# First pair's preparation reordered over queues and engines, second pair's casts placed two steps later

## The chip, the cores and the metric

The kernel runs on one core of one Trainium2 chip. A core has the engines TensorE (PE in the profile, with its weight loads PEld), VectorE (DVE), ScalarE (ACT), GpSimd (POOL) and SyncE (SP), each with its own queue of instructions in program order, and 16 DMA engines that carry out the transfers that SP, ACT and POOL issue. The metric is the device time of one execution in microseconds (us), lower is better.

## The reference

Three parts run one after the other. First an attention over B = 2 batches, H = 8 heads, S = 768 positions and D = 64 columns a head, in which a query sees only the keys of its own hash bucket (six sign bits of a projection):

```python
q_bits = (einsum('bhsd,dk->bhsk', q, proj) > 0)      # k_bits likewise
mask = q_bucket[:, :, :, None] == k_bucket[:, :, None, :]
scores = where(mask, (q @ k^T) / sqrt(D), -1e9)
attn = softmax(scores)                               # rows of 768
out = attn @ v                                       # then laid out as 1536 tokens x 512
```

Then a dense MLP, x = silu(x @ w_in) @ w_out (512 to 2048 to 512), and then a choice of one of eight experts for the tokens with x @ w_skip > 0, whose result is added to x. The change touches only the attention, and of it only the start.

## The kernel before, in words

The heads are handled in pairs: pair i has two heads, hd 0 and hd 1, and there are 8 pairs. Each pair's queries are cut in two halves of 384; a half of a pair is a unit (`units`, L367), and a unit has three blocks of 128 queries (qt) for each of the two heads. One block of one head is a step; there are 96 steps, 12 to a pair. Step 0 to 2 are hd 0 of the first unit and steps 3 to 5 its hd 1; from step 6 on heads alternate, so step 12 is hd 0 and step 13 hd 1 of pair 1 (L369, L370).

float32 products are made from float32r parts. Per pair there are four operand tiles (`prep_alloc`, L291), each with a plane for each head. With r the 64 partitions that belong to the head and o the other 64 (`own`, L296): K1 holds K's high part in r ("kh", a cast) and its low part in o ("kl"); Q1 holds Q's high part in r ("qa") and a copy of it in o ("qb"); Q2 holds Q's low part ("ql") and 24 rows of bucket marks; K2 holds a copy of K's high part ("k2") and rows of marks. `prep_op` (L303) makes each of these for one pair and head on the engine that it is given; for pairs other than the first, "k2" and "qb" are transfers that SP issues from one part of SBUF to another. `prep_proj` (L332) projects raw K and Q with four matmul groups and turns the signs into marks (tile mb, on DVE), and `prep_rows` (L343) copies the marks with SP's transfers into Q2 and K2: four for the first pair, six for the others. "scale" (L307) scales the next pair's raw K on ACT.

A step s runs: `em_S`, two matmuls over Q1 and K1 (all 128 partitions) and two over Q2 and K2 (88), into a PSUM tile of which there are two; `em_soft`, the maximum (mx, L395) and a bias (bs, L397) on DVE and the exp on ACT (L399); two steps later `em_T`, six transposes of the exp's result (L411), copied out by ACT (L414, first half) and DVE (L416, second half); and in odd steps from the middle of the next unit on `em_PV` (L425). `em_r` (L432) takes a unit's sums, transposes them, writes them out (r_d, L439) and reads them back broadcast (rb, L442, two transfers), all issued by SP.

The order of the work is written out by hand in the loop at L523. In a step it emits em_S of s, the first half of em_T of s - 2, the operations of `PRE` due in this step (the next pair's "kh" and "qa" on ACT), em_PV, em_soft, the second half of em_T, em_r, and then the operations of `POST` due (the next pair's "k2" and "qb" by SP, "kl" and "ql" on POOL), prep_rows, and raw and v loads. The index m of a step in its pair decides what is due; for the first pair (i == 0) PRE and POST have lists of their own. em_r of unit 0 falls on step 9, prep_rows of pair 1 on step 8 and its prep_proj on step 5. A queue keeps program order, and SP waits in it for the data of each transfer.

Ahead of the loop (L472 to L514) stand the constants' load (ct, by ACT), the raw loads of pair 0 head by head (k, q, k, q by SP), 29 matmuls on zeros (`em_busy`), the projection of hd 0 alone (pd, L491), the operands of hd 0 and most of hd 1, then the loads and rows.

Of the kernel before, what the change touches and what calls it, by code (L numbers as in the profile page):

```python
# [25 lines left out]
def kernel(  # L26
# [237 lines left out]
    def attention(hook):  # L264
# [11 lines left out]
        def prep_load(i):  # L276

            b, p = divmod(i, NP)
            raws[i] = [topp.tile([P, S], F32, name="raw", tag=tag, bufs=2) for tag in "kq"]
            for hd in range(2) if i == 0 else (None,):  # L280
                for t, src in zip(raws[i], (kT, qT)):
                    if hd is None:
                        nc.sync.dma_start(t, src[b, 2 * p:2 * p + 2].rearrange("h d s -> (h d) s"))
                    else:
                        nc.sync.dma_start(t[own(hd)], src[b, 2 * p + hd])
# [10 lines left out]
        def own(hd):  # L296
            return slice(hd * D, (hd + 1) * D)
# [5 lines left out]
        def prep_op(i, hd, what, eng):  # L303
# [7 lines left out]
            if what == "k2" and i:  # L311
                nc.sync.dma_start(K2[0:D, hd].bitcast(F32), K1[r, hd].bitcast(F32))
            elif what == "qb" and i:
# [26 lines left out]
        def marked(dst, ps, r):  # L340
            nc.vector.tensor_scalar(dst, ps[r], c_m[r, 0:1], c_m[r, 1:2], op0=ALU.is_gt, op1=ALU.mult)
# [133 lines left out]
        for t in mxs:  # L475
            nc.vector.memset(t, 1.0)
        nc.scalar.dma_start(ct, consts[:, 0:NC + P])
        prep_load(0)
# [10 lines left out]
        for j in (2, 3, 0):  # L489
            t = raws[0][1 - j // 2]  # L490
            nc.tensor.matmul(ps[32 * j:32 * j + 32], prj[j // 2][own(0)], t[own(0), (j % 2) * HQ:(j % 2 + 1) * HQ],  # L491
                             start=True, stop=True)
        prep_op(0, 0, "kh", nc.scalar)
        prep_op(0, 0, "qa", nc.scalar)
        prep_op(0, 0, "kl", nc.vector)
        prep_op(0, 0, "qb", nc.gpsimd)
        prep_op(0, 0, "ql", nc.gpsimd)
        prep_op(0, 0, "k2", nc.scalar)
        marked(Q2[D:NK2, 0, 0:HQ], ps, slice(0, NM2))
        for c in range(2):  # L500
            marked(K2[D:D + 2 * NB, 0, c * HQ:(c + 1) * HQ], ps, slice(64 + 32 * c, 64 + 32 * c + 2 * NB))
        prep_load(1)
        em_busy(6)
        em_S(0, (0,))
        prep_op(0, 1, "kh", nc.scalar)
        prep_op(0, 1, "qa", nc.scalar)
        prep_proj(0)
# [3 lines left out]
        prep_op(0, 1, "qb", nc.gpsimd)  # L511
# [5 lines left out]
               for c in ((1, 3, 5, 7), (2, 4, 6, 8))]  # L517
# [3 lines left out]
                for c in ((1, 2, 3, 4, 5, 7, 7, 9), (2, 3, 4, 5, 6, 7, 8, 9))]  # L521
        rbs, xs = {}, {}
        for s in range(NS + PU + 4):  # L523
# [20 lines left out]
            if s == 1:  # L544
                prep_op(0, 1, "k2", nc.scalar)
                prep_op(0, 1, "kl", nc.vector)
# [683 lines left out]
```

## Time and profile before

| what | us |
|---|---|
| median of 3 runs | 620.6 (620.07 to 621.95) |
| the profiled execution | 622.04 |
| its span, first to last instruction | 620.3 |
| PE busy | 604.2 (97%) |
| DVE busy | 465.7 (75%) |
| ACT busy | 400.7 (65%) |
| POOL busy | 167.3 (27%) |

Attention takes the first 225 us or so, the MLP follows to about 499, and the experts to the end. The engines' shares are means over all three; the change is in the first 40 us. In a view, "L385" is line 385 of the kernel, "S<-K,Q" reads: writes tile S, reads K and Q; "[1.46 <-DMA raw]" is the idle time of the engine ahead of an instruction and what ended it; SPq and ACTq are the issuing of transfers by SP and ACT. PE's matmuls are pipelined and their ends are modelled.

### The profile page before, as it was taken

To read this page: it belongs to the slowest core of one execution; us is meant where nothing else is said; L and a number is where in the kernel's file an instruction comes from. 1 tells how busy PE (TensorE), PEld (TensorE's weight loads), DVE (VectorE), ACT (ScalarE), POOL (GpSimd) and SP (SyncE) were. 2 spreads that over 40 slices of the span, in tenths; PEclk is the share of its full clock that TensorE was granted. 3 is DMA by queue.
4 is the path that set the end of the run, shared out by engine and by line. 5 is a ranking of instruction groups with operands and counts; after the bars stand their busy time and mean duration, and the time that the engine had idled before them with its cause. 6 is when DMAs were issued, how large, how long until landed. Compare 5 with 4: busy or idle time off the path is not lost.

```text
span 620.3 us, 9579 instructions
## 1 busy us (share of the span) xinstructions
PE 604.2 (97%) x3263; PEld 463.3 (75%) x3263; DVE 465.7 (75%) x861; ACT 400.7 (65%) x671; POOL 167.3 (27%) x256
## 2 busy tenths in 40 slices
PE   8899999999999999999999999999999979999996
PEld 5767667676666757788888887788888857788885
DVE  6877777888787667799747775457885469899992
ACT  6988888888877985466554333443334456888881
POOL 5535637373653143000000000020000054534101
PEclk9999999999999999999999999999999999999999
DMA  4433542524324131666423000024232349999900
GB/s 134 144 113 93 174 124 58 157 66 137 79 66 122 46 115 52 214 216 229 143 89 121 1 1 1 1 47 164 97 103 101 118 150 257 395 408 408 391 20 28
DMA packets 30978, 83.47 MB, mean 135 GB/s; under 512 B 6032, under 2 KB 9810, under 8 KB 30798
## 3 DMA queue, kind: packets, MB, share of 16 engines
q1 hardware_dynamic: 28834, 79.06, 38.6%
q0 software_dynamic: 1936, 3.65, 1.7%
q8 instruction: 26, 0.43, 0.3%
q14 instruction: 26, 0.21, 0.1%
q10 hardware_dynamic: 156, 0.11, 0.1%
HBM read 67.66 MB, written 8.50 MB: 123 GB/s over the span
## 4 chain that ended last, share of the span: by engine, by line
PE 87%; DVE 4%; ACT 3%; DMA 2%; issue 2%; POOL 1%; SPq 0%; POOLq 0%; DVEq 0%; ACTq 0%
PE ph L605 20%; PE o L648 13%; PE S L385 11%; PE T L411 10%; PE pv L425 10%; PE o L639 7%; PE eh L1046 6%; PE ey L1068 6%; ACT P L399 1%; PE tr L1024 1%; PE pj L337 1%; DVE wlo L252 1%; PE bs L472 1%; DMA w<-in_mw_dram 1%; ACT K L317 1%
## 5 line engine op out<-in xcount | busy, mean ns | idle before, releaser
L252 DVE TENSOR_TENSOR wlo<-wraw,whi 128x1024 fp32r<-128x1024 f32 x100 | 119.6, 1222 | 5.8 <-ACT whi L249 4.9
L249 ACT CAST whi<-wraw 128x1024 fp32r<-128x1024 f32 x100 | 102.7, 1050 | 20.0 <-DVE wraw L223 13.1
L399 ACT ACTIVATE P<-S,bs 128x768 f32<-128x768 f32 x96 | 95.5, 994 | 27.1 <-DVE bs L397 25.3
L611 ACT ACTIVATE g<-ph 128x512 f32<-128x512 f32 x48 | 28.6, 597 | 119.8 <-PE ph L605 113.1
L395 DVE TENSOR_REDUCE mx<-S 128x1 f32<-128x768 f32 x96 | 91.1, 949 | 11.1 <-PE S L385 8.8
L385 PE MATMUL S<-K,Q 88*128 88x384 f32 (+1 forms) x384 | 92.3, 361 | 3.1 <-ACT P L399 3.0
L411 PEld LDWEIGHTS T<-ident,P 128*128 128x128 f32 x576 | 68.1, 141 | 30.8 <-ACT PT L414 22.1
L411 PE MATMUL T<-ident,P 128*128 128x128 f32 x576 | 88.7, 277 | 0.2 <-ACT PT L414 0.2
L613 DVE TENSOR_TENSOR gl<-g,gh 128x512 fp32r<-128x512 f32 x48 | 33.6, 701 | 68.9 <-ACT gh L612 68.9
L777 POOL DMA_INDIRECT id_d<-tk,slot x12 | 12.2, 1014 | 248.1 <-DVE pre L785 245.0
L425 PE MATMUL pv<-PT,v 128*64 128x384 f32 x384 | 72.3, 498 | 0.0
L385 PEld LDWEIGHTS S<-K,Q 88*128 88x128 f32 (+1 forms) x384 | 62.7, 191 | 11.7 <-ACT P L399 5.8
L416 DVE COPY PT<-T 128x384 f32<-128x384 f32 x85 | 47.0, 553 | 22.5 <-PE T L411 22.4
L414 ACT COPY PT<-T 128x384 f32<-128x384 f32 x107 | 50.5, 479 | 7.1 <-PE T L411 6.8
L605 PE MATMUL ph<-xhi,whi 128*128 128x512 f32 x192 | 52.9, 397 | 0.0
L605 PE MATMUL ph<-xhi,wlo 128*128 128x512 f32 x192 | 51.8, 392 | 0.7 <-DVE wlo L252 0.7
L605 PE MATMUL ph<-xlo,whi 128*128 128x512 f32 x192 | 51.9, 392 | 0.0
L325 POOL TENSOR_TENSOR K<-raw,K 64x192 fp32r<-64x192 f32 x56 | 31.6, 594 | 53.9 <-ACT K L317 28.9
L661 DVE CUSTOM_DVE_ANT_0 junk<-x,gwb 128x512 bf16<-128x512 f32 x72 | 45.4, 687 | 0.0
L330 POOL TENSOR_TENSOR Q<-raw,Q 64x192 fp32r<-64x192 f32 x64 | 36.1, 592 | 28.1 <-ACT Q L320 26.4
L605 PEld LDWEIGHTS ph<-xhi,wlo 128*128 128x128 f32 x192 | 36.0, 188 | 9.0 <-DVE wlo L252 1.2
L425 PEld LDWEIGHTS pv<-PT,v 128*64 128x64 f32 x384 | 23.4, 136 | 25.7 <-issue 25.6
(173 smaller groups left out, 1045.6 us busy)
## 6 DMA issues: line engine op xcount, KB each, us to landing
wraw<-in_w_dram SPq DMA_DIRECT2D x64, 512.0 KB
w<-in_mw_dram SPq DMA_DIRECT2D x32, 512.0 KB
v<-in_vt_dram SPq DMA_DIRECT2D x8, 384.0 KB
rb<-r_d SPq DMA_DIRECT2D x32, 96.0 KB
out_dram<-x SPq DMA_DIRECT2D x12, 256.0 KB
x_d<-x SPq DMA_DIRECT2D x11, 256.0 KB
raw<-in_kT_dram SPq DMA_DIRECT2D x7, 384.0 KB
raw<-in_qT_dram SPq DMA_DIRECT2D x7, 384.0 KB
```

The source lines that it names most:

```text
L249: nc.scalar.copy(hi[:, sl], t[:, sl])
L252: eng.tensor_tensor(lo[:, sl], t[:, sl], hi[:, sl].bitcast(F32), op=ALU.subtract)
L385: nc.tensor.matmul(ps[:, c, 0:HQ], q_[0:n, hd, q0:q0 + P], k_[0:n, hd, c * HQ:(c + 1) * HQ], start=first, stop=not first)
L395: nc.vector.tensor_reduce(mx[:, 0:1], ps[:, :, 0:HQ], axis=AX.XY, op=ALU.max, negate=True)
L399: nc.scalar.activation(pt.rearrange("p (a b) -> p a b", a=2), ps[:, :, 0:HQ], AF.Exp, bias=bs_[:, 0:1], scale=bs_[:, 1:2], accum_out=st_su ...
L411: nc.tensor.transpose(ps[:, j], pt[:, k * P:(k + 1) * P], ident)
L414: nc.scalar.copy(dst, ps)
L416: nc.vector.tensor_copy(dst, ps)
L425: nc.tensor.matmul(st_pv[u][hd * D:(hd + 1) * D], vts[i][:, k, hd], st_PT[u][:, hd, k], start=(k == 0), stop=(k == KT - 1))
L605: nc.tensor.matmul(p_[:, 0:c1 - c0], w[:, k * P:(k + 1) * P], x[:, k, t0 * P + c0:t0 * P + c1], start=(q == 0), stop=(q == len(ops3) - 1))
L648: nc.tensor.matmul(acc[t], g[:, (t - t0) * P:(t - t0 + 1) * P], w[:, DM:PIECE], start=(f == 0 and q == 0), stop=(f == NF - 1 and q == 2))
L661: nc.vector.tensor_tensor_reduce(junk, xts[t], pools["gwb_t"][:, c], op0=ALU.mult, op1=ALU.add, scale=1.0, scalar=0.0, accum_out=L[:, t, c ...
```

## The change

- The loads of pair 0 come ahead of the constants' load, and the first head's q is issued by ACT instead of SP; the constants' load is now behind it in ACT's queue.
- In pair 0, "qb" of hd 0 goes from POOL to DVE and stands ahead of "kh", "qa" and "kl". The marks of K are made ahead of those of Q.
- em_busy(6) becomes em_busy(2).
- In pair 0, "k2" and "qb" of hd 1 become SP's transfers (they were ACT's, at step 1, and POOL's). Both stand ahead of prep_proj and prep_rows. "kl" of hd 1 on DVE moves from step 1 to the place ahead of prep_proj.
- For pair 1, the casts "kh", "qa", "kh", "qa" move from steps 2, 4, 6, 8 to 4, 6, 8, 9, and "k2", "kl", "qb", "ql" of both heads from steps 2, 3, 4, 5, 6, 7, 8, 9 to 4, 5, 6, 7, 8, 9, 9, 10. prep_proj and prep_rows of pair 1 and em_r stay where they are.

```diff
--- before.py
+++ after.py
@@ -282,7 +282,7 @@
                     if hd is None:
                         nc.sync.dma_start(t, src[b, 2 * p:2 * p + 2].rearrange("h d s -> (h d) s"))
                     else:
-                        nc.sync.dma_start(t[own(hd)], src[b, 2 * p + hd])
+                        (nc.scalar if hd == 0 and src is qT else nc.sync).dma_start(t[own(hd)], src[b, 2 * p + hd])
 
         def load_v(i):
             vts[i] = mainp.tile([P, KT, 2, D], F32, name="v", bufs=3)
@@ -308,9 +308,9 @@
                 return
             Q1, K1, Q2, K2 = ops[i]
             r, o = own(hd), own(1 - hd)
-            if what == "k2" and i:
+            if what == "k2" and (i or hd):
                 nc.sync.dma_start(K2[0:D, hd].bitcast(F32), K1[r, hd].bitcast(F32))
-            elif what == "qb" and i:
+            elif what == "qb" and (i or hd):
                 nc.sync.dma_start(Q1[o, hd].bitcast(F32), Q1[r, hd].bitcast(F32))
             elif what in ("kh", "k2"):
                 dst = K1[r, hd] if what == "kh" else K2[0:D, hd]
@@ -474,8 +474,8 @@
         mxs = [mainp.tile([P, 2], F32, name=f"mx{j}", bufs=1) for j in range(4)]
         for t in mxs:
             nc.vector.memset(t, 1.0)
+        prep_load(0)
         nc.scalar.dma_start(ct, consts[:, 0:NC + P])
-        prep_load(0)
         nc.vector.memset(K2s[0][D:D + 32].bitcast(F32), 0.0)
         make_identity(nc, ident)
         prep_alloc(0)
@@ -490,35 +490,37 @@
             t = raws[0][1 - j // 2]
             nc.tensor.matmul(ps[32 * j:32 * j + 32], prj[j // 2][own(0)], t[own(0), (j % 2) * HQ:(j % 2 + 1) * HQ],
                              start=True, stop=True)
+        prep_op(0, 0, "qb", nc.vector)
         prep_op(0, 0, "kh", nc.scalar)
         prep_op(0, 0, "qa", nc.scalar)
         prep_op(0, 0, "kl", nc.vector)
-        prep_op(0, 0, "qb", nc.gpsimd)
         prep_op(0, 0, "ql", nc.gpsimd)
         prep_op(0, 0, "k2", nc.scalar)
-        marked(Q2[D:NK2, 0, 0:HQ], ps, slice(0, NM2))
         for c in range(2):
             marked(K2[D:D + 2 * NB, 0, c * HQ:(c + 1) * HQ], ps, slice(64 + 32 * c, 64 + 32 * c + 2 * NB))
+        marked(Q2[D:NK2, 0, 0:HQ], ps, slice(0, NM2))
         prep_load(1)
-        em_busy(6)
+        em_busy(2)
         em_S(0, (0,))
         prep_op(0, 1, "kh", nc.scalar)
         prep_op(0, 1, "qa", nc.scalar)
+        prep_op(0, 1, "k2", None)
+        prep_op(0, 1, "qb", None)
+        prep_op(0, 1, "kl", nc.vector)
         prep_proj(0)
         prep_rows(0)
         load_v(0)
         load_v(1)
-        prep_op(0, 1, "qb", nc.gpsimd)
         prep_op(0, 1, "ql", nc.gpsimd)
         prep_op(1, 0, "scale", nc.scalar)
         nc.gpsimd.memset(K2s[1][D:D + 32].bitcast(F32), 0.0)
 
         PRE = [[(c[j], j // 2, w, nc.scalar) for j, w in enumerate(("kh", "qa", "kh", "qa"))]
-               for c in ((1, 3, 5, 7), (2, 4, 6, 8))]
+               for c in ((1, 3, 5, 7), (4, 6, 8, 9))]
 
         POST = [[(c[j], j // 4, w, None if w in ("k2", "qb") else nc.gpsimd)
                  for j, w in enumerate(("k2", "kl", "qb", "ql") * 2)]
-                for c in ((1, 2, 3, 4, 5, 7, 7, 9), (2, 3, 4, 5, 6, 7, 8, 9))]
+                for c in ((1, 2, 3, 4, 5, 7, 7, 9), (4, 5, 6, 7, 8, 9, 9, 10))]
         rbs, xs = {}, {}
         for s in range(NS + PU + 4):
             i, m = divmod(s, 2 * PU)
@@ -541,9 +543,6 @@
                 em_PV(u, k)
             if s < NS:
                 em_soft(s)
-            if s == 1:
-                prep_op(0, 1, "k2", nc.scalar)
-                prep_op(0, 1, "kl", nc.vector)
             if s < 2:
                 em_busy(4)
             if 0 <= s - 2 < NS:
```

## Rows read from the trace of the kernel before

**Rows 1.** The page, part 4: shares of the chain that ended last, by engine.
```profile
PE 87%; DVE 4%; ACT 3%; DMA 2%; issue 2%; POOL 1%; SPq 0%; POOLq 0%; DVEq 0%; ACTq 0%
```
**Rows 2.** The chain of work that ended last, 26 to 70 us: start, us, what.
```profile
by line: PE pv L425 32.7%; PE S L385 31.7%; PE T L411 31.6%; PE pj L337 3.6%; PE rT L436 0.7%; issue 0.0%
...
26.88 1.44 PE pv L425 x8
31.30 1.44 PE pv L425 x8
...
34.57 0.70 PE S L385 x4
```
**Rows 3.** Timeline of SP's queue, 0 to 80 us: start, us, transfer issued.
```profile
23.08 0.46 SPq L312 DMA_DIRECT2D K<-K  x1
26.92 0.46 SPq L314 DMA_DIRECT2D Q<-Q  x1
...
32.50 0.41 SPq L439 DMA_DIRECT2D r_d<-r  x1
35.02 1.65 SPq L442 DMA_DIRECT2D rb<-r_d  x2
36.73 0.58 SPq L289 DMA_DIRECT2D v<-in_vt_dram  x1
...
43.82 0.28 SPq L439 DMA_DIRECT2D r_d<-r  x1
45.02 1.09 SPq L442 DMA_DIRECT2D rb<-r_d  x2
46.21 0.54 SPq L314 DMA_DIRECT2D Q<-Q  x1
```
**Rows 4.** Timeline of ACT, 26 to 28.9 us.
```profile
26.06 0.83 ACT L320 CAST Q<-raw 64x768 fp32r<-64x768 f32 x1
```
**Rows 5.** DMA traffic, 22 to 28 us in 40 slices of 0.15 us.
```profile
GB/s 61 61 82 61 102 61 21 0 0 0 0 0 0 0 143 205 225 184 225 225 102 0 0 0 0 0 0 0 0 0 0 0 0 0 0 0 0 0 0 0
```
**Rows 6.** Timeline of all engines, 0 to 32 us.
```profile
0.77 0.38 ACTq L477 DMA_DIRECT2D ct<-in_consts_dram  x1
...
1.41 0.58 SPq L285 DMA_DIRECT2D raw<-in_qT_dram  x1
...
3.92 0.84 ACT L317 ACTIVATE K<-raw 64x768 fp32r<-64x768 f32 x1 [1.46 <-DMA raw<-in_kT_dram]
...
4.22 2.21 PE L491 MATMUL pd<-raw,ct 64*32 64x384 f32 x6
4.80 0.95 DVE L327 SCALAR_TENSOR_TENSOR K<-raw,K 64x768 fp32r<-64x768 f32 x1 [1.72 <-ACT K L317]
...
5.03 1.41 POOL L320 CAST Q<-raw 64x768 fp32r<-64x768 f32 x1 [3.69 <-DMA raw<-in_qT_dram]
...
7.16 1.40 DVE L341 TENSOR_SCALAR K<-pd,ct 12x384 fp32r<-12x384 f32 x2
```
**Rows 7.** The chain of work that ended last, 0 to 60 us.
```profile
6.42 0.76 PE bs L472 x6
...
9.44 0.68 DVE mb L341
...
13.57 0.84 ACT K L317
...
14.80 0.84 ACT K L317
15.65 0.73 ACT P L399
```
**Rows 8.** Busy us by engine in a stretch (instructions), granted clock, DMA share, GB/s.
```profile
10.00:26.00 16.00, 12.98 (x93) 10.85 (x91) 13.86 (x26) 14.34 (x27) 9.96 (x17) 1.00 0.48 145
```
**Rows 9.** The same view at the end of the span (PE, PEld, DVE, ACT, POOL).
```profile
614.00:615.00 1.00, 0.25 (x3) 0.05 (x1) 0.48 (x1) 0.00 (x0) 0.61 (x1) 1.00 0.00 0
...
618.00:619.00 1.00, 0.00 (x0) 0.00 (x0) 0.00 (x0) 0.00 (x0) 0.00 (x0) 0.50 0.00 0
```

## The prediction

> **What bounds the kernel now.** I read the page first: 87% of the chain that ended last is PE [rows 1]. The profiled execution took 622.04 us, 1.74 us more than its span of 620.3; the median of the three runs is 620.6. I work out a difference on the profiled execution and add it to the median. A difference under 0.3% (1.9 us) is about what a measurement of this kernel can't tell from no change.
>
> All edits lie in the first 40 us, so the chain of the start was next, and it has two parts. Until about 26.5 us it changes between PE, DVE and ACT: of the 16 us between 10 and 26 PE is busy 12.98 and ACT 14.34 (the first and fourth numbers of [rows 8]), so ACT's queue and the dependence S, maximum, exp, next S pace the steps. From the first PV on (26.88) the chain is PE alone, with 0.0% "issue" to 70 us [rows 2]. The reader should take two things from this: time saved in the first part brings everything after it forward, and a PE stall put into the second part is not won back there. I found no later stage that starts by a clock of its own: attention's end, the MLP and the experts follow in program order.
>
> Last came SP's queue, since the change moves or adds transfers there. It works and waits in order: a transfer that lacks its data holds back all behind it.
>
> **Part 1, the next pair's casts two steps later: a stall at step 13.** For the second pair (pair 1), K and Q of its second head (hd 1) were cast at steps 6 and 8; now K comes at step 8 and Q at step 9, each followed by a copy on SP ("k2", "qb"). Before, "qb" of hd 1 was issued at step 8, ahead of the six row transfers of prep_rows: Q<-Q at 26.92 us, then the rows, r_d at 32.50, rb at 35.02, the v load at 36.73 [rows 3]. After, step 8 issues "k2" and the six rows; step 9 issues r_d and both rb (em_r of unit 0 stands ahead of the POST operations of its step) and only then "qb". So "qb" takes the place that the v load has now. Behind it on SP wait a v load and raw loads of later pairs, which PE doesn't need soon. But "qb" itself is needed: from step 6 on the steps alternate heads, so step 13 is the first of pair 1 with hd 1, and its first matmul reads all 128 partitions of Q1 for hd 1, of which "qb" writes 64.
>
> The sum, in the times of before. At step 8 ACT casts K instead of Q, of the same size (26.06 to 26.89 [rows 4]), so "k2" is issued where Q<-Q was, at 26.92. Then, by the starts in [rows 3]:
> - "k2" and six rows, until r_d: 32.50 - 26.92 = 5.58
> - r_d, until rb (which reads what r_d wrote) can be issued: 35.02 - 32.50 = 2.52
> - both rb: 36.73 - 35.02 = 1.71; "qb" is issued at 36.73
> - issue to landing: K<-K, also 192 KB, issued at 23.08 [rows 3], moved its data from 24.10 to 25.15 (slices 15 to 21, of 0.15 us each, of [rows 5]), so 2.1 at least; r_d's 2.52 is the other end; I take 2.2, nearer to the row of the same size.
>
> It lands at 38.9. Before, PE began the S of step 13 at 34.57 [rows 2]. The stall is 4.3 to 4.7, taken as 4.4 us. Step 13 stands at the head of PE's queue: transposes, PV and all later steps wait behind it. What is late next: step 13's softmax follows its S, but PE then has the transposes, PV and projection of the next steps in hand, so no second stall follows. The shortest form takes r_d's wait from the next unit, where rb follows r_d by 45.02 - 43.82 = 1.20 (and Q<-Q follows rb, at 46.21 [rows 3]): 1.3 less, 3.1 us. I keep 2.52, because here six row transfers go just ahead of r_d in both kernels.
>
> **Part 2, less on ACT in steps 1 to 3.** Pair 0's "k2" (13.57) and the next pair's first cast (14.80), 0.84 us each, stand on the chain just ahead of the third exp (15.65) [rows 7]. Gone from there, the third exp can start earlier. But four casts still stand ahead of the tenth exp, two of them (steps 8 and 9) now close together, and ACT has little room in this stretch [rows 8]. What lasts is at most the one cast that became a transfer, 0.84; at least nothing. I take 0.25, nearer to nothing because ACT now idles at the third exp and is full again from the next cast on. The new transfers of pair 0's hd 1 cost nothing: five ACT casts of 0.84 from 3.92 [rows 6] make their sources ready by 7.3 and 8.1, SP is otherwise idle until mb is made (9.44 + 0.68 [rows 7]), so with 2.1 to 2.5 each they land by 11; step 3's S, which needs them, came after the ACT copy at 13.57 that they replace. Without that cover of some 2.5 us each microsecond late would cost one.
>
> **Part 3, the start itself.** Four warm-up matmuls fewer: six take 0.76 us on the chain [rows 7], so 0.5 is saved, if DVE keeps up. DVE now runs the q copy, K's low half (0.95), K's two marks (1.40 together), Q's mark, the second K low half (0.95, now ahead of mb) and mb [rows 6, 7]. The copy is not in the trace on DVE: K's low half, of the same 64x768, gives 0.95 as one end, half of it 0.5 as the other; I take 0.85, nearer to the row. What it runs past 4.80, when K's low half can start, pushes the whole list: mb comes 0.5 earlier than at 9.44 with the short copy, 0.15 with the long one. Against it stands the constants' load: ct is first in ACT's queue now (0.77); after, it stands behind a 192 KB load, and the first projection (4.22) needs it: from 0 to 0.6 later, one load's issue (0.58) [rows 6]. POOL loses a copy of 1.41 [rows 6], which lets its Q work start sooner but isn't on the chain. Together 0.2 us, bounds -0.4 and 0.5.
>
> An earlier q is worth little here: Q's cast follows K's (3.92 to 4.76 [rows 6]) on ACT anyway, and K isn't loaded sooner. The Trainium skill, "DMA: Bandwidth & Descriptors", section "Issuing engines are not separate DMA queues", says that a second issuing engine saves only the time to issue, because all share the same DMA engines; by that K could even land later, beside q, and the start would give nothing. That lies inside the bounds just given.
>
> **The sum.** Parts 2 and 3 bring everything up to step 8, with the cast that starts part 1, 0.45 us forward (bounds -0.4 and 1.35). The stall costs 4.4. Net 3.95: 620.6 + 3.95 = 624.5 us (626.0 for an execution like the profiled one). Bounds: 4.3 - 1.35 = 2.95 and 4.7 + 0.4 = 5.1, so 623.5 to 625.7 for this case.
>
> **The rivals.**
> - *The stall, and a lower clock behind it.* PE would idle 4.4 us. After the last matmul (614.25) the granted clock is still 1.00 to 615 and 0.50, the lower of its two levels, from 618 on [rows 9]: it had fallen within 3.75 us. No row shows it rise, so I bound the price by work: two steps of PE take 31.30 - 26.88 = 4.4 us [rows 2], one 2.2, and at 1.2 GHz that much more. From half a step to one: 1.1 to 2.2, taken as 1.8: 626.3 us. The Trainium skill, "TensorE: Matmul & The Clock Gate", Part 1, says that the throttled state is the default and activity releases it. The end of this trace agrees (1.00 to 0.50 in idleness).
> - *A shorter stall,* with r_d's wait as in the next unit: 3.1 - 0.45 = 2.65, so 623.3 us.
> - *Not slower: ACT's queue is the whole delay of the start.* PE idles 16 - 12.98 = 3.0 us between 10 and 26 [rows 8]. If the later casts let PE close all of it, with the start's 0.5, step 8 comes 3.5 earlier and the net is 4.4 - 3.5 = 0.9: 621.5 us, within 0.3%. It decides from a gain of 2.5 us on; beyond 6.3 it would be faster by over 0.3%. Against it: the casts move by two steps only, and ACT stays full.
> - *The change doesn't do what I read:* "qb" isn't behind rb, or lands before PE gets there. Then parts 2 and 3 alone count: 620.15 us; at their upper bounds 619.25, still within 0.3%.
>
> **How the numbers follow.** Stall at full clock 0.60 (624.5); with the lower clock 0.20 (626.3); shorter stall 0.07 (623.3); not slower through ACT 0.06 (621.5, 0.01 of it faster); no stall 0.07 (620.15, 0.02 of it faster). Slower by over 0.3%: 0.60 + 0.20 + 0.07 = 0.87, less 0.02 for lower edges, 0.85; same 0.12; faster 0.03. The range takes the likeliest case, most of the lower-clock case and the shorter stall, 622.6 to 626.8; the not-slower cases and the upper edge of the clock case, under 2 in 10, are left out.
>
> **What would show it.** Part 1: in SP's queue of the changed kernel a Q<-Q directly behind two rb near 36 us, and one PE idle stretch of about 4 us near 34 us, ahead of the S of step 13 and ended by DMA Q. A granted clock under 1.00 behind it means the lower clock. Part 2: the third exp about 1 us earlier than 15.65, but the first PV under 1 us earlier than 26.88. Part 3: mb 0.1 to 0.5 earlier than 9.44; ct's landing, by the first projection against 4.22. I am wrong if no S waits for that DMA, or if the first PV comes over 2.5 us earlier.

## The result: 1.5% slower, and the profile after

The changed kernel took 631.41 us (median of 5, 628.55 to 632.06) against 621.51 for the kernel before (5 runs beside it): 1.0147 times as long, interval 1.0126 to 1.0168, or 9.9 us. The sign was forecast; the size was not (3.95), and the time lies 4.6 us above the range. The profiled execution is the fastest of the five: 628.55 us, span 626.8, 6.5 more than the span of before. The other four took 2.4 to 3.5 us longer, and their mean granted clock was 0.984 to 0.987 instead of 0.995, so this trace shows only a part of the loss; another execution of the same kernel (e13) shows more of it.

Page of after, part 4: shares of the chain that ended last [answers rows 1].

```profile
PE 85%; DMA 5%; DVE 2%; ACT 2%; issue 2%; POOL 1%; SPq 1%; ACTq 0%; POOLq 0%; DVEq 0%
```

PE is down from 87% and DMA up from 2% to 5%, some 20 us. Of these, 8.7 lie in the first 40 us: 4.21 for the constants at the very start, and 1.59 for r_d and 2.93 for Q<-Q at step 13. The other 11.6 are two transfers among the experts (at 519.66 and 526.09 us), where the chain takes another way and nothing is lost: from the experts' first matmul to the end of the span it is 121.3 us before and 121.6 after.

**Step 13.** Timeline of SP's queue of after: start, us, transfer issued [rows 3].

```profile
27.43 0.46 SPq L312 DMA_DIRECT2D K<-K  x1
...
33.02 0.41 SPq L439 DMA_DIRECT2D r_d<-r  x1
34.63 1.14 SPq L442 DMA_DIRECT2D rb<-r_d  x2
35.82 0.58 SPq L314 DMA_DIRECT2D Q<-Q  x1
36.45 0.59 SPq L289 DMA_DIRECT2D v<-in_vt_dram  x1
```

Timeline of PE of after; in brackets the idle time ahead of an instruction and what ended it.

```profile
38.88 0.94 PE L385 MATMUL S<-K,Q 128*128 128x384 f32 x4 [3.41 <-DMA Q<-Q]
39.66 0.49 PE L411 MATMUL T<-ident,P 128*128 128x128 f32 x3
40.08 2.78 PE L425 MATMUL pv<-PT,v 128*64 128x384 f32 x8
...
43.63 0.85 PE L337 MATMUL pj<-raw,ct 128*32 128x384 f32 x8
```

The same of PE of before, for steps 10 and 13 and the projection behind step 13:

```profile
28.66 0.95 PE L385 MATMUL S<-K,Q 128*128 128x384 f32 x4
...
34.33 0.95 PE L385 MATMUL S<-K,Q 128*128 128x384 f32 x4
...
35.54 1.51 PE L425 MATMUL pv<-PT,v 128*64 128x384 f32 x8
...
37.45 0.85 PE L337 MATMUL pj<-raw,ct 128*32 128x384 f32 x8
```

Q<-Q ("qb") is directly behind the two rb, in the place forecast, and the S of step 13 waits 3.41 us for it. Behind the wait eight pv matmuls take 2.78 us, where before eight took 1.51. The busy table of after says why: us, busy us (instructions) of PE, PEld, DVE, ACT, POOL, then granted clock, DMA share and GB/s.

```profile
34.00:38.00 4.00, 1.48 (x12) 1.20 (x10) 2.15 (x4) 2.61 (x6) 0.00 (x0) 1.00 0.38 100
38.00:42.00 4.00, 3.12 (x13) 1.75 (x15) 1.12 (x2) 1.81 (x3) 0.52 (x1) 0.77 0.86 301
42.00:46.00 4.00, 4.00 (x26) 2.21 (x23) 1.82 (x3) 1.11 (x4) 1.71 (x4) 0.80 0.22 49
```

In half-microsecond stretches the clock is 0.50, the lower of its two levels, from 40.5 to 43.5. Before it was 1.00 throughout here.

**The start.** Timeline of after, all engines, lines of PE, DVE, ACT and ACT's queue [rows 6].

```profile
0.77 0.56 ACTq L285 DMA_DIRECT2D raw<-in_qT_dram  x1
...
1.37 0.60 ACTq L478 DMA_DIRECT2D ct<-in_consts_dram  x1
...
5.20 0.84 ACT L317 ACTIVATE K<-raw 64x768 fp32r<-64x768 f32 x1 [1.91 <-DMA raw<-in_kT_dram]
5.60 0.25 DVE L484 TENSOR_SCALAR ct<-ct 128x12 f32<-128x12 f32 x2 [2.89 <-DMA ct<-in_consts_dram]
5.88 0.55 DVE L320 CAST Q<-raw 64x768 fp32r<-64x768 f32 x1
...
5.90 1.50 PE L491 MATMUL pd<-raw,ct 64*32 64x384 f32 x6 [1.61 <-DVE ct L484]
```

The constants' load was issued 0.6 us later than before, and its data were used at 5.60; in the kernel before the same DVE instruction (L484) ran at 2.83. The first projection waits for it and starts at 5.90 instead of 4.22 [rows 6]. K, which I had called not sooner, came 1.3 us later in this trace: 5.20 against 3.92. In the other two traces of the changed kernel it was on time (3.97 and 4.01), and there the constants were later still, as the table below shows.

### The profile page after: what moved, and what is told of

Same layout as the page of the kernel before. It is cut to its first block, busy times and chain, and to the rows that moved or that the text cites. A ratio compares the mean times of both kernels' runs of the same rounds, so it can differ in the third digit from the quotient of the medians.

```text
span 626.8 us, 9574 instructions
## 1 busy us (share of the span) xinstructions
PE 606.6 (97%) x3259; PEld 464.1 (74%) x3259; DVE 466.8 (74%) x862; ACT 400.1 (64%) x670; POOL 166.2 (27%) x254
## 4 chain that ended last, share of the span: by engine, by line
PE 85%; DMA 5%; DVE 2%; ACT 2%; issue 2%; POOL 1%; SPq 1%; ACTq 0%; POOLq 0%; DVEq 0%
PE ph L604 20%; PE o L647 13%; PE S L385 11%; PE T L411 10%; PE pv L425 10%; PE o L638 7%; PE eh L1045 6%; PE ey L1067 6%; ACT P L399 1%; PE tr L1023 1%; PE pj L337 1%; DMA id_d<-tk,slot 1%; DMA eidr<-id_d 1%; DMA r_d<-r 1%; DMA ct<-in_consts_dram 1%
## 5 line engine op out<-in xcount | busy, mean ns | idle before, releaser
L425 PE MATMUL pv<-PT,v 128*64 128x384 f32 x384 | 73.6, 506 | 0.0
```

The lines of the kernel that those rows point to most:

```text
L425: nc.tensor.matmul(st_pv[u][hd * D:(hd + 1) * D], vts[i][:, k, hd], st_PT[u][:, hd, k], start=(k == 0), stop=(k == KT - 1))
```

## The experiments

Each kernel was timed beside the kernel before on the same chip; the ratio has a 95% interval. Where a difference in us stands, it is between the two medians of one measurement; the ratio isn't that of these two medians, and need not give quite the same. Three questions were open: whether the place in SP's queue makes the stall (and all of it), what the start costs and why, and what the lower clock behind each costs.

### The changed kernel twice more (e1, e13)

No edit; the first text is that of e1, the second that of e13.

> The changed kernel once more, for a second profile and its times beside the experiments. Main theory: PE stalls 3.4 to 4.4 us at the S of step 13 for the qb transfer that SP issues behind rb, a lower clock behind that stall costs 1.9 us, and the late constants cost some 0.6 us; that makes 6.2 us over before. Executions of this kernel were up to 3 us slower still, at a mean granted clock of 0.984 to 0.987 instead of 0.995. Rival B: there the clock is lower at the start too, because PE idles 1.6 us for the constants right after its first 3.3 us of matmuls; then a profile of such an execution shows a granted clock under 1.00 before 14 us. Rival C: the low stretch behind the stall is longer there; then it shows over 4 us of 0.50 behind 38 us. Either: 6 to 10 us over before.

> The changed kernel once more, for a trace of another execution. Theory: it differs from the other two only in when the constants land (5.6 to 7 us) and in where the granted clock is at 0.50: behind step 13 in all of them, and in some also at the start (before 18 us) or in the routing of the experts (510 to 530 us). 6 to 10 us over before. Rival: the executions differ in something else; then a trace with the same landing and clock differs by over 1 us.

Measured: e1 629.77, 1.0127 (1.0106 to 1.0148); e13 631.16, 1.0134 (1.0104 to 1.0163). The traces put the loss down step by step. Each column from the third on says how much later than in the trace of before an event comes, by its start in PE's timeline (in the trace of before: step 10's S at 28.66, step 13's at 34.33, the projection at 37.45; the 34.57 of [rows 2] is where the chain enters that S).

| trace | constants used at | S of step 10 | S of step 13 | projection behind step 13 | span |
|---|---|---|---|---|---|
| after | 5.60 | +0.6 | +4.6 | +6.2 | +6.5 |
| e1 | 6.58 | +2.0 | +5.9 | +7.5 | +7.6 |
| e13 | 6.22 | +3.0 | +6.9 | +8.5 | +9.6 |

The differences along a line are the causes: the start (0.6 to 3.0), the stall (3.9 in all three), the lower clock behind the stall (1.6 in all three), the rest of the program (0.1 to 1.1). The start is net of a relief: from step 2's S to that of step 10 it is 16.12 us in the trace of before and 15.4 to 15.5 in these three, some 0.7 less. The rest lies in code that no edit touches: from the experts' first matmul to the end it takes 121.1 to 123.6 us over all the traces, so differences of an us or two in it belong to the execution. Only the start varies much, and e13 shows with what. Busy table of e13, columns as above:

```profile
6.00:8.00 2.00, 1.06 (x8) 0.26 (x8) 1.74 (x4) 1.98 (x3) 2.00 (x4) 1.00 1.01 339
8.00:10.00 2.00, 1.22 (x6) 0.70 (x10) 1.95 (x3) 0.91 (x2) 1.93 (x3) 0.52 0.76 183
...
16.00:18.00 2.00, 2.00 (x10) 1.90 (x9) 1.44 (x3) 1.23 (x4) 0.00 (x0) 0.50 0.63 160
18.00:20.00 2.00, 2.00 (x14) 1.93 (x14) 1.45 (x4) 1.16 (x3) 0.00 (x0) 0.92 0.98 340
```

From 8 to 18 us PE works at the lower level, after it had stood still for the constants and again for DVE. That is 2.3 us more at the start than in the trace of after (3.0 against 0.6), with constants only 0.6 later, and the mean clock of this execution, 0.986, is that of the four slower runs of the changed kernel. So the median of 631.41 probably holds both, a late start and a lower clock behind it; one trace of each measurement can't show more. That trace of e1, and that of after, have 1.00 in this view through the start.

### The lists alone, and the rest alone (e4, e2)

e4 is the kernel before with only the later casts; e2 is the changed kernel with the old lists.

```diff
 # e4, on the kernel before
-               for c in ((1, 3, 5, 7), (2, 4, 6, 8))]
+               for c in ((1, 3, 5, 7), (4, 6, 8, 9))]
...
-                for c in ((1, 2, 3, 4, 5, 7, 7, 9), (2, 3, 4, 5, 6, 7, 8, 9))]
+                for c in ((1, 2, 3, 4, 5, 7, 7, 9), (4, 5, 6, 7, 8, 9, 9, 10))]
 # e2, on the changed kernel: the same four lines, the other way round
```

> The kernel before with only the second pair's casts and copies moved to the later steps. Main theory: by the queue's order alone qb of hd 1 is issued behind rb near 36.5 us, PE waits for it at step 13 for 3.5 to 4.5 us, and the lower clock behind it costs 1.9: 5 to 6.5 us over before. Rival (the stall needs the other parts of the change too, or ACT's relief pays for it): under 2 us over before. Rival C: 7 to 9 us.

> The changed kernel with the second pair's casts and copies at their old steps; all else as changed. Main theory: no PE wait for Q<-Q near 35 us and no low clock behind it; what is left is the start with the late constants, 0 to 1 us over before. Rival B (the wait for the constants lowers the clock at the start): 1 to 4 us over before, with a granted clock under 1.00 before 14 us. Rival C: 0 to 1 us over before at a mean clock of 0.998. If the casts' place is not the cause: 6 to 10 us over before.

e4: 628.06, 1.0101 (1.0080 to 1.0121), 6.1 us. e2: 625.88, 1.0072 (1.0055 to 1.0088), 3.95 us. Timeline of PE of e4:

```profile
38.94 1.62 PE L385 MATMUL S<-K,Q 128*128 128x384 f32 x4 [4.50 <-DMA Q<-Q]
40.35 0.84 PE L411 MATMUL T<-ident,P 128*128 128x128 f32 x3
41.13 2.83 PE L425 MATMUL pv<-PT,v 128*64 128x384 f32 x8
...
44.44 0.85 PE L337 MATMUL pj<-raw,ct 128*32 128x384 f32 x8
```

With the start of before untouched, the S of step 13 starts 4.4 us later than the 34.57 of [rows 2], the 4.4 of the prediction (4.6 later by the timeline). That the sum comes out so well is partly luck, since its terms were off in opposite senses, as told below. PE had come to it 0.4 us sooner (step 10 at 28.27 against 28.66), so the stall itself is 5.0 here, against 3.9 in the changed kernel. The projection behind it is 7.0 later (44.44 against 37.45), so 2.4 us went to the lower clock, more than the rival's 1.8. So more than half of the loss is the stall and what it does to the clock. The other part, 3.95 us in e2, has nothing to do with the lists. Timeline of e2, DVE and PE:

```profile
6.93 0.64 DVE L484 TENSOR_SCALAR ct<-ct 128x12 f32<-128x12 f32 x2 [4.23 <-DMA ct<-in_consts_dram]
...
7.63 1.50 PE L491 MATMUL pd<-raw,ct 64*32 64x384 f32 x6 [3.33 <-DVE ct L484]
```

The constants come 4.1 us late here, and the granted clock is 0.50 from 8 to 14. I had given the constants nothing worse than 0.6.

### Is the place in SP's queue the whole stall? (e5, e14)

Both are e4 with one copy out of its place. e5 issues "qb" of pair 1's hd 1 from ACT; e14 leaves it with SP and puts r_d and rb of unit 0 behind it.

```diff
 # e5, on e4
-                nc.sync.dma_start(Q1[o, hd].bitcast(F32), Q1[r, hd].bitcast(F32))
+                (nc.scalar if (i, hd) == (1, 1) else nc.sync).dma_start(Q1[o, hd].bitcast(F32), Q1[r, hd].bitcast(F32))
 # e14, on e4
-                if k == (1 if u + 1 < len(units) else 3):
+                if k == (1 if u + 1 < len(units) else 3) and s != 9:
                     rbs[u] = em_r(u)
...
+                if s == 9:
+                    rbs[u] = em_r(u)
```

> The kernel before with the later casts, as in the run with the lists alone (6.1 us over before), but the one transfer qb of pair 1's hd 1 is issued from ACT's queue, so that it doesn't stand behind the rows, r_d and rb on SP. Main theory (the place in SP's queue is the whole cause): it lands near 31 us, no wait at step 13, no low clock: -0.5 to +0.7 us against before. Rival (the casts themselves come too late, or crowd ACT): still 3 us or more over before.

> The lists alone (6.1 us over before), with em_r of unit 0 emitted behind the copies of step 9, so that qb of hd 1 stands behind the six row transfers on SP but ahead of r_d and both rb. Theory (the wait is the sum of the prediction's queue places): qb is issued 4.2 us sooner, as soon as the rows are issued, lands near 34.6 us, and PE waits 0 to 0.6 us at step 13: -0.5 to +1 us against before. Rival (the rows alone, or ACT's crowded queue, hold it as long): 3 us or more over before.

e5: 622.20, 1.0001 (0.9987 to 1.0014). e14: 622.25, 1.0004 (0.9986 to 1.0023). Both are level with before; the 6.1 us of e4 are gone. Timeline of e14, SP's queue and PE:

```profile
31.92 0.53 SPq L314 DMA_DIRECT2D Q<-Q  x1
32.55 0.43 SPq L439 DMA_DIRECT2D r_d<-r  x1
...
35.04 0.94 PE L385 MATMUL S<-K,Q 128*128 128x384 f32 x4 [0.67 <-DMA Q<-Q]
35.25 1.12 SPq L442 DMA_DIRECT2D rb<-r_d  x2
```

The copy is issued 3.7 us sooner than in e4 (35.62) and the wait falls from 4.50 to 0.67, while the six row transfers still stand ahead of it. What held the copy was the wait of rb for r_d and rb itself. A wait of 0.67 leaves the granted clock at 1.00, and the whole loss goes with it.

### What does the clock behind the stall cost? (e6, e9)

e4 with matmuls on zeros ahead of step 13's S, 38 in e6 and 76 in e9; they write the S tile that the following S overwrites.

```diff
             ps = st_S[s]
+            if s == 13:
+                for _ in range(76):
+                    nc.tensor.matmul(ps[:, 0, 0:P], busy, busy, start=True, stop=True)
```

> The lists alone again, with 38 matmuls on zeros put ahead of step 13's S, into the PSUM tile that this S overwrites, so that PE is busy while it waits for qb (some 4.2 us). Their products are not used. Main theory (lower clock is a cost of its own behind the stall): the granted clock stays at 1.00 and the time falls by 1.5 to 2.7 us against the lists alone: 3.7 to 4.6 us over before. Rival (the clock costs nothing, all is waiting): 6 us over before as without them.

> The lists alone with 76 instead of 38 matmuls on zeros ahead of step 13's S (38 lasted only 2.28 us, PE still idled 3.0 us and the clock still fell to 0.50). 76 should last 4.3 us and cover the whole wait. Their products are not used. Main theory (the lower clock behind the stall is a cost of its own): granted clock 1.00 from 33 to 50 us, PV behind the stall 1.44 us for 8 matmuls instead of 2.4 to 2.8, and the transfer's wait itself left: 3.7 to 4.7 us over before, against 6.1 for the lists alone. Rival (the clock costs nothing): 6 us or more over before.

e6: 630.65, 1.0132 (1.0106 to 1.0159), 8.5 us. e9: 628.62, 1.0120 (1.0098 to 1.0142), 6.5 us. In e6 the 38 took 2.28 us only, a wait of 3.00 remained, and the clock fell behind it all the same, so e6 decides nothing; 2.3 us of its profiled execution were lost among the experts. In e9 the 76 cover the wait. Timeline of PE of e9:

```profile
32.73 4.41 PE L384 MATMUL S<-busy 128*128 128x128 bf16 x76
...
37.32 0.93 PE L388 MATMUL S<-K,Q 128*128 128x384 f32 x4 [0.18 <-DMA Q<-Q]
...
38.51 1.51 PE L428 MATMUL pv<-PT,v 128*64 128x384 f32 x8
...
40.43 0.85 PE L337 MATMUL pj<-raw,ct 128*32 128x384 f32 x8
```

The copy is as late as in e4 (step 13's S starts 10.6 us behind step 10's, against 10.7), the clock stays at 1.00, and from step 13's S to the projection it is 3.11 us, as in the kernel before (3.12), instead of 5.50 in e4. In the traces, then, the lower clock costs 1.6 (after, e1, e13) to 2.4 us (e4). The times don't show it: e9's median is not below e4's (628.06), and its 6.5 us are what was set down ahead for the rival, though its runs have the higher mean clock (0.996 to 0.998 against 0.992 and 0.993). The trace tells where the gain went. The projection behind step 13 comes 4.0 us sooner in e9 than in e4, 2.4 of it from the clock and 1.6 because the clock at the start rose sooner in that execution. At the experts' first matmul 3.8 of it are left (501.99 against 505.78), at the end of the span 2.1: the experts' part took 122.8 us in e9 and 121.1 in e4. No edit touches that part, and its scatter is as large as the price looked for. So the price of the clock behind the stall is shown by traces alone.

### Which part of the start is late? (e3, e12, e8)

e3 is the changed kernel with the constants ahead of q in ACT's queue; e12 is e2 with the constants first in SP's queue and q alone in ACT's; e8 is e2 with pair 1's raw loads moved behind the first projection.

```diff
 # e3, on the changed kernel
-        prep_load(0)
         nc.scalar.dma_start(ct, consts[:, 0:NC + P])
+        prep_load(0)
 # e12, on e2
+        nc.sync.dma_start(ct, consts[:, 0:NC + P])
         prep_load(0)
-        nc.scalar.dma_start(ct, consts[:, 0:NC + P])
 # e8, on e2
-        prep_load(1)
         em_busy(2)
...
         prep_proj(0)
+        prep_load(1)
```

> The changed kernel with the constants' load first in ACT's queue again, ahead of the first head's q; all else as changed. The first projection should start near 4.2 us instead of 5.9. Main theory: the stall at step 13 stays: 3.4 to 4.4 us less some 0.5 us of gain in the start, plus 1.9 us of lower clock: 4.5 to 6 us over before. Rival B: the same 4.5 to 6 us, with all executions near a mean clock of 0.995. Rival C: 7 to 9 us in the executions with a mean clock of 0.985.

> The changed kernel with the casts at their old steps, and the constants' load first in SP's queue instead of second in ACT's; the first head's q stays alone in ACT's queue. Theory (a transfer is late when it is second in ACT's queue, behind one of 192 KB): constants by 3 us, q by 5 us, first projection between 4.2 and 5.1 us, and 1 to 2.5 us over before, as for the rest alone. Rival (any transfer in ACT's queue beside SP's is late): q lands after 6 us, and 3 us or more over before.

> The changed kernel with the casts at their old steps (3.95 us over before), and pair 1's two raw loads of 384 KB moved behind prep_proj, so that SP has only three loads of 192 KB beside ACT's two. Theory R1 (ACT's second transfer lands late because SP's backlog shares the DMA engines): the constants land by 5.0 us instead of 6.9, less time lost: 1 to 2.5 us over before. Rival R2 (ACT's queue is late by itself, whatever SP has queued): constants at 5.6 to 6.9 us as now and 3 to 4.5 us over before.

e3: 632.04, 1.0159 (1.0123 to 1.0195), no better than the change itself and above all that was forecast for it. e12: 625.40, 1.0064 (1.0045 to 1.0083). e8: 626.35, 1.0065 (1.0044 to 1.0087). Neither gains on e2's 1.0072; both come out by their rivals, not by the theory. Timeline of DVE of e3:

```profile
2.93 0.25 DVE L484 TENSOR_SCALAR ct<-ct 128x12 f32<-128x12 f32 x2 [0.22 <-DMA ct<-in_consts_dram]
6.61 0.55 DVE L320 CAST Q<-raw 64x768 fp32r<-64x768 f32 x1 [3.42 <-DMA raw<-in_qT_dram]
```

Timeline of e12, DVE and ACT:

```profile
4.19 0.55 DVE L320 CAST Q<-raw 64x768 fp32r<-64x768 f32 x1 [1.00 <-DMA raw<-in_qT_dram]
4.95 0.84 ACT L317 ACTIVATE K<-raw 64x768 fp32r<-64x768 f32 x1 [2.31 <-DMA raw<-in_kT_dram]
```

In e3 the constants are on time and q is the late one (6.61). So it isn't the size of the constants' load or its target: whichever transfer is second in ACT's queue, with SP's loads beside it, is usable only at 5.5 to 7.0 us. In the kernel before q was second in SP's queue instead, and usable at 5.03 [rows 6]. In e12 the tiles come as its theory had them (constants at 2.94, q alone in ACT's queue at 4.19, the first projection at 5.06), and the time is still 3.3 us over: K, issued behind the constants at 1.21 instead of 0.77, is 1.0 us later than the 3.92 of [rows 6], and from 12 to 18 us the clock is 0.50. Through this stretch the DMA engines are full: in the trace of after their share is 0.92, 1.10 and 1.02 in the three stretches of 2 us from 2 to 8, in that of before 0.95, 1.03 and 0.94. Reordering moves the delay from one tile to another, and K, q and ct are all wanted at once. In e8 the constants still come at 5.55, though the DMA engines are busy only until about 6 there, so pair 1's loads are not, or not alone, what they queue behind. Why the second transfer in ACT's queue is served so late is open: no run tells its place in the queue from its place among all the loads issued.

### What remains with the constants first (e7, e11, e10)

e7 is the changed kernel with old lists, constants first and q back with SP: what is left is the q copy on DVE, the marks' order, hd 1's copies by DMA, the second "kl" ahead of mb and em_busy(2). e11 undoes the last two. e10 is e2 with twice the warm-up ahead of the first projection.

```diff
 # e7, on the changed kernel (beside the old lists)
-                        (nc.scalar if hd == 0 and src is qT else nc.sync).dma_start(t[own(hd)], src[b, 2 * p + hd])
+                        nc.sync.dma_start(t[own(hd)], src[b, 2 * p + hd])
...
-        prep_load(0)
         nc.scalar.dma_start(ct, consts[:, 0:NC + P])
+        prep_load(0)
 # e11, on e7
-        em_busy(2)
+        em_busy(6)
...
-        prep_op(0, 1, "kl", nc.vector)
...
+            if s == 1:
+                prep_op(0, 1, "kl", nc.vector)
 # e10, on e2
-        em_busy(29)
+        em_busy(60)
```

> The changed kernel with the casts at their old steps, the constants first and alone in ACT's queue, and the first head's q by SP again; left of the change are the q copy on DVE, K's marks first, two warm matmuls instead of six, and pair 0's hd 1 copies by transfers. Theory (the start is lost only through ACT's second transfer landing late): first projection at 4.2 us, granted clock 1.00 throughout, and 0 to 1 us faster than before. Rival (the other start edits cost too, by DVE's longer list or fewer warm matmuls): 1 us or more slower than before, with mb later than 9.44 us.

> The rest of the change alone (1.76 us over before), but with six warm matmuls again and the K low half of hd 1 at step 1 again. Left of the change: the q copy on DVE, K's marks first, and hd 1's copies by transfers. Theory (DVE's list ahead of the first maximum, and PE's gaps, cost those 1.76 us): the first maximum starts near 9.5 us instead of 10.25, and the time is -0.8 to +0.5 us against before. Rival (the copy on DVE or the transfers cost): 1.5 us or more over before.

> The changed kernel with the casts at their old steps (3.95 us over before), with 60 instead of 29 matmuls on zeros at the start, so that PE is busy up to 6 or 7 us while the constants are on their way. Theory (half of the start's loss is the lower clock that follows PE's idle time): matmuls at the full rate by 8 us, 1.5 to 2.5 us over before. Rival (all of it is the late constants and DVE's longer list): 3.5 to 4.5 us over before, as without them.

e7: 623.91, 1.0022 (1.0009 to 1.0035). e11: 622.87, 1.0013 (0.9998 to 1.0028). e10: 626.80, 1.0073 (1.0047 to 1.0098). Busy table of e7, from 10 to 18 us:

```profile
10.00:12.00 2.00, 0.53 (x6) 0.23 (x4) 1.97 (x4) 0.23 (x1) 1.94 (x4) 0.82 0.29 62
12.00:14.00 2.00, 1.09 (x3) 1.09 (x4) 0.70 (x2) 1.91 (x4) 1.08 (x1) 0.50 0.12 28
...
16.00:18.00 2.00, 2.00 (x10) 1.90 (x9) 1.28 (x2) 1.63 (x4) 1.47 (x3) 0.50 0.87 307
```

The same stretches of e11:

```profile
10.00:12.00 2.00, 1.50 (x14) 1.07 (x12) 1.80 (x4) 0.44 (x1) 1.95 (x3) 1.00 0.26 55
12.00:14.00 2.00, 1.31 (x9) 1.28 (x10) 1.74 (x4) 1.69 (x4) 0.20 (x1) 1.00 0.11 28
...
16.00:18.00 2.00, 1.74 (x12) 1.65 (x13) 1.63 (x4) 2.00 (x7) 1.56 (x3) 1.00 0.88 295
```

In e7 the first matmuls of S run at full rate (two in 0.59 us at 6.61, against 0.99 in e11; there they waited for ACT's K, so the two warm-up matmuls in place of six saved nothing), PE then has 0.53 us of work between 10 and 12, and the clock is low until 18. In e11 it stays at 1.00 in this view. Timeline of PE, the S of step 2, first in e7 and then in e11:

```profile
12.91 1.65 PE L385 MATMUL S<-K,Q 128*128 128x384 f32 x4 [2.38 <-ACT P L399]
...
12.69 0.97 PE L385 MATMUL S<-K,Q 128*128 128x384 f32 x4 [1.18 <-ACT P L399]
```

The wait ahead of this S goes with the clock in the traces: it is 2.0 to 2.4 us in e7, e10, e12 and e15, which then read 0.50, and 1.2 to 1.4 in before, e4, e5, e6, e11 and e16, which stay at 1.00. The short work between 10 and 12 alone doesn't go with it: e6 has 0.57 us there and stays at 1.00. In e7 the wait is longer because step 0's first maximum starts at 10.17 only, behind "kl" (8.59) and mb (9.58) in DVE's queue; in e5, where that "kl" comes later, it starts at 8.71. So the "kl" ahead of mb is the likelier cause, but e11 takes back the warm-up with it, and no run parts the two. Together they cost about 1 us (1.8 against 0.8; the intervals overlap, so this is likely and not shown). Both kernels missed their theories: e7 was to be up to 1 us faster, and in e11 the first maximum was to start near 9.5 and starts at 10.30.

In e10 PE works on zeros until 6.18, then stands for 1.47 us until the first projection at 7.65, which takes 0.84 us instead of 1.50. The clock falls later than in e2, to 0.50 from about 15 to 21 us, behind a wait of 2.02 ahead of step 2's S, and the time is not better than e2's. So more warm-up ahead of the late constants wins nothing: the lower clock comes behind the next wait.

### Both causes undone, and the best of the parts (e15, e16)

e15 is the changed kernel with q back on SP, the constants first and "qb" of pair 1's hd 1 issued by ACT. e16 is the kernel before with the later casts, that "qb" by ACT, and hd 1's copies of pair 0 by DMA: what of the change could help ACT, without the rest.

```diff
 # e15, on the changed kernel
-                        (nc.scalar if hd == 0 and src is qT else nc.sync).dma_start(t[own(hd)], src[b, 2 * p + hd])
+                        nc.sync.dma_start(t[own(hd)], src[b, 2 * p + hd])
...
+                (nc.scalar if (i, hd) == (1, 1) else nc.sync).dma_start(Q1[o, hd].bitcast(F32), Q1[r, hd].bitcast(F32))
...
-        prep_load(0)
         nc.scalar.dma_start(ct, consts[:, 0:NC + P])
+        prep_load(0)
 # e16, on the kernel before (beside the later casts and that "qb" by ACT)
+        prep_op(0, 1, "k2", None)
+        prep_op(0, 1, "qb", None)
         prep_proj(0)
...
-        prep_op(0, 1, "qb", nc.gpsimd)
...
-                prep_op(0, 1, "k2", nc.scalar)
```

> The changed kernel with its two suspected causes undone and all else kept, the later casts too: the constants first and alone in ACT's queue with the first head's q by SP, and qb of pair 1's hd 1 issued by ACT. Theory (these two account for nearly all): 0 to 1.8 us over before, as the rest alone. Rival (the two do not account for it): 3 us or more over before.

> The kernel before with two edits of the change alone: pair 0's hd 1 copies as transfers (less on ACT and POOL), and the later casts with qb of pair 1's hd 1 issued by ACT. The start stays as it was, with its six warm matmuls and its order on DVE. Theory (part 2 of the prediction is right, and lasts where nothing else is lost): 0.3 to 1 us faster than before. Rival (ACT's relief is given back by step 9): no difference, within 0.3 us.

e15: 624.96, 1.0043 (1.0023 to 1.0063). e16: 622.35, 1.0001 (0.9986 to 1.0015). In e15 two causes are gone and, against the 9.5 us of e13 beside it, 6.2 us with them; 3.3 stay, the mark set for the rival and more than the 1.8 of e7, and its trace has the same lower clock from 14 to 17 us. Between 1.8 and 3.3 this remainder isn't settled. In e16 the projection behind step 13 comes 0.5 us earlier than before (36.98 against 37.45), and the median is level; its interval, 0.9 us to either side, can't tell such a gain from none. No version here beats the kernel before.

## Why the prediction was wrong, point by point

- **The sum against one trace.** Of e13's 9.6 us the forecast had 3.95. The 5.65 between them are the start, 3.0 lost in place of 0.45 won (3.45), the lower clock (1.6) and the rest of the program (1.1), less a stall 0.5 shorter.
- **What bounds the kernel: held.** PE wins nothing back behind the start: in the changed kernel all of the lag at the projection reaches the span, with 0.1 to 1.1 us more, in e4 all but 0.4.
- **Part 1: the mechanism, the place and, against the start of before, the size held.** e4 gives +4.4 at step 13. The terms were off in opposite senses: in e4 r_d to rb took 2.44 (forecast 2.52), both rb 1.19 and not 1.71, issue to the end of the wait 3.3 and not 2.2; in after 1.61, 1.19 and 3.1. That these cancel is luck. The 2.1 was read from the slices in which another copy moved its data; in e14 the data of this one move until 34.2 to 34.4 and PE's wait ends at 35.04, 0.6 to 0.9 us behind that. In the changed kernel the stall comes to 3.9, net of the start, where e4 has 5.0 counted in the same way; 0.8 of that is r_d to rb, shorter there than in e4. That "no second stall follows" held.
- **The lower clock behind the stall: the rival was the rule.** It stands behind the stall in every trace of the changed kernel and of e4, with 1.6 to 2.4 us against my 1.8, and I gave it a chance of 0.20. I had the rows in which the clock falls while PE stands idle behind its last matmul [rows 9] and a forecast stall longer than that idleness; by these two it belonged in the likeliest case. The Trainium skill, "TensorE: Matmul & The Clock Gate", Part 1, has the throttled state as the default and activity as what releases it. The traces agree in direction (0.50 behind the waits of 3.41 and 4.50 us, 1.00 behind that of 0.67). With this case alone the time would have been 626.3, still 5 us short. By the profiled execution of after alone, the stall (3.9) and the clock (1.6) make 5.5 of the 6.5 us.
- **Part 3: the step that failed.** I bounded the constants' delay by "one load's issue", 0 to 0.6 us; it was 2.8 us in after, 3.4 in e13 and 4.1 in e2. With the stretch behind them counted in, that made the start 0.6 to 3.0 us slower instead of somewhat faster. No run shows the 0 to 0.6 that I took from an issue time: the constants were issued 0.6 later and used 2.8 to 4.1 later, while the DMA engines were full. Their share of 0.94 to 1.03 from 2 to 8 us stood in the trace of before and I didn't read it. A bound that holds in these traces is the end of that burst, some 5 us later than 2.83 (the share is 0.02 from 8 us on). The Trainium skill, "DMA: Bandwidth & Descriptors", section "Issuing engines are not separate DMA queues", has the transfers of all issuers interleave on the same 16 DMA engines. The traces agree in part: beside ACT's q K is used at 4.95 to 5.27 in the traces of after, e8 and e12, but at 3.95 to 4.12 in those of e1, e2, e3, e10 and e13, which is no later than where SP issues q (3.90 to 4.20). I had put that down as lying inside bounds that were too narrow.
- **The price of a late start.** 2.8 us of delay cost 0.6 in after and 3.0 in e13. Part of it is covered by the relief of 0.7 us up to step 10 and by work that waited for other things; in e13 part is added by the clock that is low from 8 to 18 us. The prediction had a price for PE idle at step 13 and none for PE idle at the start.
- **Part 3, the warm-up.** No run shows the 0.5 us. In e7 the first S waits for K by ACT, at 6.61, and starts no sooner than with six warm-up matmuls in e5 and e6 (6.64 and 6.47). What two in place of six do to the clock isn't shown by themselves, since e11 changes "kl" with them.
- **Part 3, the DVE copy** took 0.55 us, the short end (0.83 in e2, where POOL worked beside it), and mb came at 10.91 instead of 9.44 all the same, since DVE's list waited for the constants and has the second "kl" ahead of it. But that list isn't what set mb before. DVE of before waits there:

```profile
9.44 0.68 DVE L341 TENSOR_SCALAR mb<-pj,ct 128x384 fp32r<-128x384 f32 x1 [0.88 <-PE pj L337]
```

So a shorter list could bring mb forward only as far as PE's projection came sooner. In e11, with the constants on time and that "kl" back at step 1, mb is at 9.46, again ended by PE's projection.

- **Part 2: the sense held in the traces, the size is too small for the times.** 0.25 us were forecast. The stretch from step 2's S to that of step 10 is 0.6 to 0.7 shorter with the later casts, and 0.3 of it is given back by step 13 in e5 and e16; e16's projection is 0.5 earlier, its median level within 0.9 us. The rival "not slower through ACT's queue" is out: it needed 2.5 us. "The change doesn't do what I read" is out too.

## What to carry to other kernels

An operation that moves by a step also changes its place in the queue that issues it: list what in that queue waits for data, and price the new place with those waits. Where the DMA engines are full, ask when that burst ends: here a transfer put second came 2.8 to 4.1 us later for an issue 0.6 later, and loads brought forward in one queue made others late. Price a new idle stretch of PE for itself and for the clock behind it: here those of 3.4 to 4.5 us at step 13 were each followed by the lower level, and so were those of 2.0 to 2.4 at step 2, while one of 0.7 was not. The start can hold such a stretch as well.

## What the runs showed of the hardware

- A transfer second in ACT's queue, issued at 1.4 us while SP issued five loads by 4.0, was usable at 5.5 to 7.0 us (after, e1, e2, e3, e8, e10, e13); the constants, first in the same queue, at 2.8 to 2.9. Nothing in the issue times shows this.
- The granted clock of a view reads 1.00 from the first microsecond on, but the matmuls say otherwise: the 29 on zeros at the start take 3.27 us, 113 ns each, and the 76 of e9, of the same shape, 4.41 us, 58 ns each. PE starts at the lower level, and the duration of a known matmul is the safer clock. The Trainium skill's "TensorE: Matmul & The Clock Gate", Part 1, has the throttled state as the default, and that agrees.
- When the clock rises differs by execution with the same instructions ahead of it: e4 and e5 don't differ in the first 25 us, yet the S of step 2 starts at 11.09 in the trace of e5 and at 12.78 in that of e4, behind matmuls that ran at the higher level sooner. That moves an execution by 1.7 us, about half of the 3.3 us over which the five of the kernel before spread. The mean clock of an execution tells little of this: the trace of e8 has a mean of 0.999 and still a step 2's S of 1.65 us, the lower level.
- The clock also fell far from any edit: in e6 it was 0.50 from 518 to 524 us, in the experts, where no other trace that I read there (before, after, e4, e9, e13) leaves 1.00.
